# Cosformer attention and SwiGLU: the first batch's denominators computed as one-column products, and the order of the start changed

## The chip, the cores and the metric

The kernel runs on one core of a Trainium2 chip. The core has a matrix engine (TensorE; PE in the profile, with its weight loads on a row of their own, PEld), a vector engine (VectorE, DVE), a scalar engine (ScalarE, ACT), a general engine (GpSimd, POOL) and a queue engine that only issues transfers (SyncE, SP). Each engine works through its own instructions in the order in which the program issues them; engines wait for one another through semaphores. TensorE writes to PSUM, which has eight banks of 512 fp32 columns. The metric is the device time of one execution in microseconds.

## The reference

Attention without softmax for 8 batches, 8 heads, 576 positions and a head size of 64, and behind it a gated feed-forward layer on 4608 rows of 512:

```python
q_p = phi(q, cos_w, sin_w)          # [relu(x)*cos, relu(x)*sin], 128 features
k_p = phi(k, cos_w, sin_w)
kv = np.einsum('bhsf,bhsd->bhfd', k_p, v)
z = np.sum(k_p, axis=2)
num = np.einsum('bhsf,bhfd->bhsd', q_p, kv)
den = np.einsum('bhsf,bhf->bhs', q_p, z)[..., None] + 1e-06
x = num / den                       # heads side by side: rows of 512
xn = x / sqrt(mean(x * x) + 1e-6) * rms_g
out = (silu(xn @ w_gate) * (xn @ w_val)) @ w_out
```

The inner width of the feed-forward layer is 1536. Inputs and output are fp32.

## The kernel before

The feed-forward layer is most of the work: for each block of 512 rows, 12 steps of four gate and four value matmuls (`gval_mm`, L556), SiLU on ScalarE, the product of gate and value on VectorE (L576), and then 48 output matmuls (`out_mm`, L579). Attention of the batches that follow is slipped into these steps. For the first batch there is no block to hide behind, and its order is written out by hand, line by line (L608 to L760); the schedule is manual, so that the order of the calls is the order on each engine. The change lies in that stretch.

In it, batch 0 is handled in these pieces:

- `k_phi` makes the features of k in nine chunks of 64 positions (two halves of the heads stand in the partitions 0 to 63 and 64 to 127, so that a chunk holds four pairs of heads, `hp`, and two groups `g`). VectorE makes the cosine half, ScalarE the sine half of chunks 0 to 7.
- `z0_pe(c)` (L407) adds up the features of a chunk: two matmuls of 64 rows, a matrix of ones against 512 columns. `z0_copy` and `z0_turn` (L415, L418) bring the sums, which lie in a row, into a column: two copies and eight matmuls of one column.
- `g_spread` (L231) spreads the gain `rms_g` over the partitions, three small matmuls for each of four column groups; `gb` is its copy in SBUF.
- `kv0_pe(hp)` (L426) multiplies features by v: 18 matmuls of 64 rows and 64 columns for a pair of heads, the two groups by turns. They fill 64 of 65 columns of each head; the 65th holds the denominator's sum. All four pairs of a group share one bank (`heads0`, in psG). `kvz0_evac` copies a bank to SBUF.
- `q0_phi(eng, j, part)` (L323) makes the features of q tile j (128 rows; four tiles), in two instructions of 256 columns, `i` = 0 and 1, on one engine. `q_tr_pe` transposes a tile on TensorE (eight transposes), and `q0_tr_evac` copies it from PSUM.
- `nd0_pe(j)` (L455) multiplies tile j by the k-v matrices, eight matmuls of 65 columns into both banks of psA, and adds epsilon to the denominators with two matmuls more (L464). `nd_post` divides on VectorE: a reciprocal (L487) and a product (L499).
- `x_sq` sums the squares on ScalarE (L515) and raises them to -1/2 on GpSimd (L520); `x_norm` scales on VectorE (L527), `x_tr_pe` transposes (L546) and `x_tr_evac` copies to `xnT`.
- `unit_mm` (L648) is the first feed-forward work, on one or two tiles at a time.
- `filler(n, bank)` (L601) issues n matmuls of 512 columns on a tile of zeros; nobody reads their result.

Weights, q, k and v of the first batches are loaded by GpSimd's queue, in the order of their calls; the first k by SP's queue.

Of the kernel before, what the change touches and what calls it, by code (L numbers as in the profile page):

```python
# [9 lines left out]
FP32 = mybir.dt.float32  # L10
BF16 = mybir.dt.bfloat16
AF = mybir.ActivationFunctionType
ALU = mybir.AluOpType
# [4 lines left out]
def kernel(  # L18
# [11 lines left out]
    nc = tc.nc  # L30
    B, H, S, D = q.shape
    DM = H * D
    DFF = moe_w_gate.shape[1]
    P = 128
    TB = 512
    HP = H // 2
# [92 lines left out]
    def raw_q0(i):  # L129
        part = raw_tile("q", 0)[:, i * HP * 4 * D : (i + 1) * HP * 4 * D]  # L130
        return part.rearrange("p (hp e) -> p hp e", hp=HP)
# [99 lines left out]
    def g_spread(bank, t):  # L231
        for i in range(3):
            nc.tensor.matmul(  # L233
                bank[:, t * P : (t + 1) * P], lhsT=sel[:, t, :], rhs=g3[:, i, :],
                start=(i == 0), stop=(i == 2),
            )
# [47 lines left out]
    def copy(eng, o, i):  # L284
        if eng is A:
            A.copy(out=o, in_=i)  # L286
        else:
            eng.tensor_copy(out=o, in_=i)  # L288

    def phi(eng, out_ap, in_ap, scale):  # L290
        if eng is A:
            A.activation(out=out_ap, in_=in_ap, func=AF.Relu, scale=scale)  # L292
        else:
            eng.tensor_scalar(  # L294
                out=out_ap, in0=in_ap, scalar1=scale, scalar2=0.0, op0=ALU.mult, op1=ALU.max
            )
# [15 lines left out]
    def qp_of(key):  # L312
        if key not in qp_tiles:
            qp_tiles[key] = four.tile([P, H, F], BF16, name="qp", tag="qp")
        return qp_tiles[key]
# [4 lines left out]
        phi(eng, qp_of((b, j))[:, :, o], raw_q(b)[:, :, j * D : (j + 1) * D], f(9 + j))  # L320


    def q0_phi(eng, j, part):  # L323
        o = slice(0, D) if part == 0 else slice(D, F)
        f = cos_of if part == 0 else sin_of
        for i in range(2):
            c = (2 * j + i) % 4
            phi(
                eng, qp_of((0, j))[:, HP * i : HP * i + HP, o],
                raw_q0(j // 2)[:, :, c * D : (c + 1) * D], f(2 * j + i),  # L330
            )

    def q0_tr_evac(eng, j, bank):
        src = bank.bitcast(BF16).rearrange("p (i h s) -> p i h s", i=2, h=H)
# [24 lines left out]
    def q_tr_pe(b, j, bank):  # L359
        t = qp_of((b, j))  # L360
        dst = bank.bitcast(BF16).rearrange("p (h s) -> p h s", h=H)
        for h in range(H):
            nc.tensor.transpose(dst[:, h, :], t[:, h, :], ident[:, :])  # L363
# [36 lines left out]

    zbank = [psC[1], psV[1]]
    zrow = one.tile([1, 2, HP * F], BF16, name="zrow")
    heads0 = [b[:, 0 : HP * E].rearrange("p (hp e) -> p hp e", e=E) for b in psG]

    def z0_pe(c):  # L407
        for g in range(2):
            lo, hi = 64 * g, 64 * g + 64
            nc.tensor.matmul(  # L410
                zbank[g][:, :], lhsT=ones[lo:hi, :], rhs=kp[lo:hi, c, :, :],
                start=(c == 0), stop=(c == NC - 1),
            )

    def z0_copy(eng, g):  # L415
        copy(eng, zrow[:, g, :], zbank[g][0:1, :])

    def z0_turn():  # L418
        for hp in range(HP):
            for g in range(2):  # L420
                nc.tensor.matmul(
                    heads0[g][:, hp, D:E], lhsT=zrow[:, g, hp * F : (hp + 1) * F],
                    rhs=ones[0:1, 0:1], start=False, stop=False, skip_group_check=True,
                )

    def kv0_pe(hp):  # L426
        for c in range(NC):
            for g in range(2):
                lo, hi = 64 * g, 64 * g + 64
                nc.tensor.matmul(  # L430
                    heads0[g][:, hp, 0:D], lhsT=kp[lo:hi, c, hp, :],
                    rhs=vv0[lo:hi, hp, c * D : (c + 1) * D],
                    start=(hp == 0 and c == 0), stop=(hp == HP - 1 and c == NC - 1),
                    skip_group_check=True,
                )

    def kvz0_evac(eng, g):
        if 0 not in kvzs:
            kvzs[0] = six.tile([P, 2, HP * E], BF16, name="kvzs", tag="kvzs")
        copy(eng, kvzs[0][:, g, :], psG[g][:, 0 : HP * E])  # L440

    def kvz_evac(eng, b):
        kvzs[b] = six.tile([P, 2, HP * E], BF16, name="kvzs", tag="kvzs")
# [8 lines left out]
            )  # L452


    def nd0_pe(j):  # L455
        for h in range(H):
            g, hp = h % 2, h // 2
            nc.tensor.matmul(
                heads[:, g, hp, :], lhsT=qpT[:, h, j * P : (j + 1) * P],
                rhs=kvzs[0][:, g, hp * E : (hp + 1) * E],  # L460
                start=(hp == 0), stop=False, skip_group_check=True,
            )
        for g in range(2):
            nc.tensor.matmul(  # L464
                heads[:, g, :, D], lhsT=eps_ones[:, :], rhs=eps_rows[:, :],
                start=False, stop=True, skip_group_check=True,
            )

    def nd_tails_pe(pair):
# [25 lines left out]
    def nd_div(b, j):  # L495
        xt = xts[count["x"] % NXT]
        count["x"] += 1
        rec = rec_of[(b, j)]
        V.tensor_tensor(  # L499
            out=xt[:, 0:DM].rearrange("p (hp g d) -> p g hp d", g=2, d=D),  # L500
            in0=heads[:, :, :, 0:D],
            in1=rec[:, :, :].unsqueeze(3).to_broadcast([P, 2, HP, D]),
            op=ALU.mult,
        )
        x_of[(b, j)] = xt

    def nd_post(b, j):
        nd_rec(b, j)
        nd_div(b, j)
# [91 lines left out]
    def filler(n, bank):  # L601
        for _ in range(n):
            nc.tensor.matmul(  # L603
                bank[:, :], lhsT=warm[:, 0:P], rhs=warm[:, :], start=True, stop=True
            )


    qbank = [psV[0], psA[:, 0, :], psV[0], psV[1]]  # L608
    g_parts()
    filler(10, psC[1])  # L610
    for c in range(NC):
        k_phi(V, 0, c, 0)
        k_phi(A if c < 8 else V, 0, c, 1)
        z0_pe(c)
        if c < NDT:
            g_spread(psC[0], c)
    kv0_pe(0)
    kv0_pe(1)
    for j in range(2):
        q0_phi(V, j, 0)  # L620
        q0_phi(A, j, 1)
        q_tr_pe(0, j, qbank[j])
    z0_copy(V, 1)
    z0_copy(A, 0)
    q0_tr_evac(V, 0, qbank[0])
    q0_tr_evac(A, 1, qbank[1])
    V.tensor_copy(out=gb[:, :], in_=psC[0][:, :])
    z0_turn()
    kv0_pe(2)
    kv0_pe(3)  # L630
    kvz0_evac(A, 0)
    kvz0_evac(V, 1)

# [44 lines left out]

    HALF = DM // 2
    lo, hi = (0, NDT // 2), (NDT // 2, NDT)
    filler(2, psC[1])
    nd0_pe(0)
    q0_phi(V, 2, 0)
    q0_phi(G, 3, 0)
    q0_phi(A, 2, 1)
    q0_phi(A, 3, 1)
    filler(2, psC[1])
    nd_post(0, 0)  # L690
    q_tr_pe(0, 2, qbank[2])
    filler(1, psC[1])
    x_sq(0, 0)
    load_w(wv, moe_w_val, 8, NNT)
    nd0_pe(1)
    q0_tr_evac(V, 2, qbank[2])
    filler(2, psC[1])
    q_tr_pe(0, 3, qbank[3])
    nd_post(0, 1)
    filler(1, psC[1])  # L700
    nd0_pe(2)
    x_sq(0, 1)
    load_q(1, eng=G)
    load_kv("v", 1, eng=G)
# [3 lines left out]
    filler(1, psG[1])  # L708
    x_tr_pe(0, 0, psC[1], hi)
    x_tr_evac(A, 0, 0, psC[0], lo)  # L710
    x_tr_evac(V, 0, 0, psC[1], hi)
    q0_tr_evac(A, 3, qbank[3])
    x_norm(0, 1)
# [226 lines left out]
```

## Time and profile before

| | |
|---|---|
| three runs | 323.29, 323.61, 324.15 us; median 323.61 |
| the profiled execution | 323.16 us, its span 321.4 us |
| TensorE | busy 317.2 us, 99% of the span, 2310 matmuls |
| VectorE | 184.5 us, 57% |
| ScalarE | 166.2 us, 52% |
| GpSimd | 40.4 us, 13% |
| transfers | 53.76 MB, mean 167 GB/s |

The profile is of one execution. The span runs from its first to its last instruction; the execution's time has 1.76 us more around it. A matmul's row has the duration of the single instruction, and matmuls overlap: two that start 0.06 us apart each have a duration of 0.22. The busy time of TensorE therefore tells little of how far it is from its peak, and the distance between starts tells more. The chain that ended last is followed back from the last instruction; what stands on it sets the end.

### The profile page before, as it was taken

What the parts mean: (1) busy time and instruction counts of PE and PEld (TensorE: products, weight loads), DVE (VectorE), ACT (ScalarE), POOL (GpSimd) and SP (SyncE); (2) the same over time, 40 slices, a digit from 0 to 9 for tenths busy, and PEclk for the clock granted to TensorE, in tenths of its full rate; (3) what the DMA queues carried; (4) which work ended last, traced back from release to release, by engine and by line L of the source; (5) the groups of instructions that cost most, each with busy time, mean ns of one, the idle gap of its engine ahead of it and who ended that gap; (6) DMA issues with size and microseconds to landing.
All of it is one profiled execution on the core that took longest, in us unless ns stands there. A gap on an engine that the chain in (4) does not pass through costs nothing.

```text
span 321.4 us, 6061 instructions
## 1 busy us (share of the span) xinstructions
PE 317.2 (99%) x2310; PEld 162.5 (51%) x2310; DVE 184.5 (57%) x382; ACT 166.2 (52%) x322; POOL 40.4 (13%) x79
## 2 busy tenths in 40 slices
PE   8999999999999999999999999999999999999996
PEld 2689564554454445444544445544544444444444
DVE  7976858668447773777457645781676034204410
ACT  5766756754584466554744575446543333223321
POOL 9771211002001100011001100100011000000000
PEclk9999999999999999999999999999999999999999
DMA  7999999987999989999799859995522500041002
GB/s 234 238 274 268 279 330 159 262 183 189 227 224 203 194 260 189 234 250 168 159 190 230 195 161 200 198 217 162 99 58 42 116 33 0 0 102 31 1 35 98
DMA packets 80091, 53.76 MB, mean 167 GB/s; under 512 B 52234, under 2 KB 74046, under 8 KB 80062
## 3 DMA queue, kind: packets, MB, share of 16 engines
q1 hardware_dynamic: 73110, 41.25, 62.0%
q0 software_dynamic: 6944, 12.13, 15.5%
q8 instruction: 18, 0.29, 0.4%
q14 instruction: 11, 0.09, 0.1%
q10 hardware_dynamic: 8, 0.00, 0.0%
HBM read 37.83 MB, written 9.44 MB: 147 GB/s over the span
## 4 chain that ended last, share of the span: by engine, by line
PE 97%; DVE 1%; ACT 0%; issue 0%; POOL 0%; ACTq 0%
PE psC L579 27%; PE psG L556 27%; PE psV L556 27%; PE psA L449 2%; PE psV L648 2%; PE psG L579 2%; PE psG L648 2%; PE psA L387 2%; PE psC L603 1%; PE psC L410 1%; PE psA L394 1%; PE psA L474 0%; PE psV L363 0%; PE psG L430 0%; PE psC L546 0%; PE psC L233 0%
## 5 line engine op out<-in xcount | busy, mean ns | idle before, releaser
L576 DVE TENSOR_TENSOR hT<-psV,sg 128x512 bf16<-128x512 f32 x100 | 68.9, 689 | 97.7 <-PE psV L556 65.4
L575 ACT ACTIVATE sg<-psG 128x512 f32<-128x512 f32 x100 | 59.2, 592 | 62.3 <-PE psG L556 61.0
L556 PE MATMUL psV<-xnT,wv 128*128 128x512 bf16 x352 | 90.3, 379 | 0.0
L556 PE MATMUL psG<-xnT,wg 128*128 128x512 bf16 x352 | 90.3, 379 | 0.0
L579 PE MATMUL psC<-wo,hT 128*128 128x512 bf16 (+1 forms) x408 | 88.9, 376 | 0.0
L579 PEld LDWEIGHTS <-hT 128*128 128x128 bf16 x456 | 43.0, 98 | 47.8
L556 PEld LDWEIGHTS <-wv 128*128 128x128 bf16 x400 | 39.1, 98 | 47.2
L556 PEld LDWEIGHTS <-wg 128*128 128x128 bf16 x400 | 36.9, 98 | 39.8 <-DVE xnT L288 0.4
L520 POOL TENSOR_TENSOR rs<-ms,mhalf 128x1 f32<-128x1 f32 x36 | 20.5, 571 | 194.6 <-ACT scr L515 194.4
L286 ACT COPY osb<-psC 128x512 f32<-128x512 f32 x32 | 18.8, 586 | 49.9 <-PE psC L579 49.9
L515 ACT ACTIVATE scr<-xt 128x513 bf16<-128x513 f32 x36 | 22.8, 634 | 25.1 <-DVE xt L499 24.4
L527 DVE SCALAR_TENSOR_TENSOR xn<-xt,rs,gb 128x512 bf16<-128x512 f32 (+1 forms) x37 | 27.0, 731 | 9.9 <-POOL rs L520 9.8
L292 ACT ACTIVATE kp<-raw,tab 128x256 bf16<-128x256 f32 (+2 forms) x51 | 28.8, 607 | 2.2 <-DMA raw<-in_k_dram 2.2
L499 DVE TENSOR_TENSOR xt<-psA,rec 128x512 f32<-128x512 f32 x36 | 24.9, 691 | 1.2
L292 ACT ACTIVATE qp<-raw,tab 128x512 bf16<-128x512 f32 (+1 forms) x36 | 23.4, 666 | 1.0 <-DMA raw<-in_q_dram 0.8
L294 DVE TENSOR_SCALAR kp<-raw,tab 128x256 bf16<-128x256 f32 (+2 forms) x53 | 19.9, 423 | 0.5 <-DMA raw<-in_k_dram 0.5
L294 DVE TENSOR_SCALAR qp<-raw,tab 128x512 bf16<-128x512 f32 (+1 forms) x34 | 15.4, 466 | 4.2 <-DMA raw<-in_q_dram 4.2
L449 PEld LDWEIGHTS <-qpT 128*128 128x128 bf16 x224 | 10.5, 97 | 6.7 <-issue 0.7
L556 PE MATMUL psV<-xnT_tail,wv 128*128 128x512 bf16 x48 | 12.3, 379 | 0.0
L556 PE MATMUL psG<-xnT_tail,wg 128*128 128x512 bf16 x48 | 12.3, 379 | 0.0
L449 PE MATMUL psA<-kvzs,qpT 128*128 128x65 bf16 x224 | 11.4, 193 | 0.0
L288 DVE CAST vv<-raw 116x1280 bf16<-116x1280 f32 (+1 forms) x13 | 10.5, 807 | 1.1 <-DMA raw<-in_v_dram 1.1
(100 smaller groups left out, 178.2 us busy)
## 6 DMA issues: line engine op xcount, KB each, us to landing
out_dram<-osb SPq DMA_DIRECT2D x27, 256.0 KB, 2.3
raw<-in_q_dram SPq DMA_DIRECT2D x6, 1024.0 KB, 9.3
raw<-in_k_dram SPq DMA_DIRECT2D x5, 1120.0 KB, 8.5
raw<-in_v_dram SPq DMA_DIRECT2D x5, 1120.0 KB, 9.5
raw<-in_k_dram POOLq DMA_DIRECT2D x2, 1152.0 KB, 19.4
raw<-in_v_dram POOLq DMA_DIRECT2D x2, 1152.0 KB, 16.0
out_dram<-osb SPq DMA_DIRECT2D x17, 128.0 KB, 2.7
wg<-in_moe_w_gate_dram POOLq DMA_DIRECT2D x3, 512.0 KB, 13.6
```

The source lines that it names most:

```text
L286: A.copy(out=o, in_=i)
L292: A.activation(out=out_ap, in_=in_ap, func=AF.Relu, scale=scale)
L294: eng.tensor_scalar(out=out_ap, in0=in_ap, scalar1=scale, scalar2=0.0, op0=ALU.mult, op1=ALU.max)
L449: nc.tensor.matmul(heads[:, g, hp, :], lhsT=qpT[:, h, j * P : (j + 1) * P], rhs=kvzs[b][:, g, hp * E : (hp + 1) * E], start=True, stop=True,)
L499: V.tensor_tensor(out=xt[:, 0:DM].rearrange("p (hp g d) -> p g hp d", g=2, d=D), in0=heads[:, :, :, 0:D], in1=rec[:, :, :].unsqueeze(3).to ...
L515: A.activation(out=scr[:, :], in_=xt[:, 0 : DM + 1], func=AF.Square, scale=1.0 / math.sqrt(DM), accum_out=ms[:, :],)
L520: G.tensor_tensor(out=rs[:, :], in0=ms[:, :], in1=mhalf[:, :], op=ALU.pow)
L527: V.scalar_tensor_tensor(out=xn_of[(b, j)][:, c], in0=x_of[(b, j)][:, c], scalar=rs_of[(b, j)][:, :], in1=gb[:, c], op0=ALU.mult, op1=ALU. ...
L556: nc.tensor.matmul(bank[:, cols[0] : cols[1]], lhsT=w[:, t, n * P : (n + 1) * P], rhs=x[:, t, cols[0] : cols[1]], start=(t == 0), stop=(t ...
L575: A.activation(out=sg[:, :], in_=g[:, 0:TB], func=AF.Silu)
L576: V.tensor_tensor(out=hT[:, n, :], in0=v[:, 0:TB], in1=sg[:, :], op=ALU.mult)
L579: nc.tensor.matmul(bank[:, 0 : cols[1] - cols[0]], lhsT=hT[:, n, j * P : (j + 1) * P], rhs=wo[:, n, cols[0] : cols[1]], start=(n == 0), st ...
```

## The change

The sums of the features of k are formed in a column from the start: `z0_pe(c)` now takes the features as weights and a single column of ones as the moving operand, eight matmuls for a chunk, each into the 65th column of its head. `z0_copy` and `z0_turn` are gone. The heads of pairs 0 and 1 stay in psG, those of pairs 2 and 3 go to psV[1] and psC[1], so that the k-v matrices are copied in two halves for each group. Tile 0 is multiplied and divided in two halves, the first between the k-v products of pairs 0, 1 and those of pairs 2, 3 (`nd0_half`, new). The spreads of the gain come together ahead of the features of k, five fillers stand between the chunks, and the copy of `gb` moves from VectorE to ScalarE. `q0_phi` takes one half of 256 columns at a time; tile 1 gives VectorE three of four, and tiles 2 and 3 are dealt anew between VectorE, ScalarE and GpSimd, which now has one piece instead of two. VectorE's copy of q tile 2 and the product of tile 2 come after the first transposes of x. The transposes of q tile 1 use psC[0] instead of psA.

```diff
-    def q0_phi(eng, j, part):
+    def q0_phi(eng, j, part, i):
...
-    def z0_copy(eng, g):
-        copy(eng, zrow[:, g, :], zbank[g][0:1, :])
-
-    def z0_turn():
         for hp in range(HP):
             for g in range(2):
+                lo, hi = 64 * g, 64 * g + 64
                 nc.tensor.matmul(
-                    heads0[g][:, hp, D:E], lhsT=zrow[:, g, hp * F : (hp + 1) * F],
-                    rhs=ones[0:1, 0:1], start=False, stop=False, skip_group_check=True,
+                    heads0(hp, g)[:, D:E], lhsT=kp[lo:hi, c, hp, :], rhs=ones[lo:hi, 0:1],
+                    start=(hp % 2 == 0 and c == 0), stop=False, skip_group_check=True,
                 )
...
-    def kvz0_evac(eng, g):
+    def kvz0_evac(eng, g, half):
...
-        copy(eng, kvzs[0][:, g, :], psG[g][:, 0 : HP * E])
+        bank = (psG[g], (psV[1], psC[1])[g])[half]
+        copy(eng, kvzs[0][:, g, 2 * E * half : 2 * E * half + 2 * E], bank[:, 0 : 2 * E])
...
+    def nd0_half(half):
+        hps = slice(2 * half, 2 * half + 2)
...
+        V.reciprocal(out=rec0[:, :, hps], in_=heads[:, :, hps, D])
+        V.tensor_tensor(
+            out=x_of[(0, 0)][:, 0:DM].rearrange("p (hp g d) -> p g hp d", g=2, d=D)[:, :, hps],
+            in0=heads[:, :, hps, 0:D],
+            in1=rec0[:, :, hps].unsqueeze(3).to_broadcast([P, 2, 2, D]), op=ALU.mult,
+        )
...
-    qbank = [psV[0], psA[:, 0, :], psV[0], psV[1]]
+    qbank = [psV[0], psC[0], psV[0], psV[1]]
+    half0, half1 = (0, HP // 2), (HP // 2, HP)
     g_parts()
-    filler(10, psC[1])
+    filler(10, psV[0])
+    for t in range(NDT):
+        g_spread(psC[0], t)
     for c in range(NC):
         k_phi(V, 0, c, 0)
         k_phi(A if c < 8 else V, 0, c, 1)
         z0_pe(c)
-        if c < NDT:
-            g_spread(psC[0], c)
+        if 2 < c < NC - 1:
+            filler(1, psV[0])
+    for part in range(2):
+        q0_phi(V, 0, part, 0)
+        q0_phi(A, 0, part, 1)
+    q_tr_pe(0, 0, qbank[0])
     kv0_pe(0)
     kv0_pe(1)
-    for j in range(2):
-        q0_phi(V, j, 0)
-        q0_phi(A, j, 1)
-        q_tr_pe(0, j, qbank[j])
-    z0_copy(V, 1)
-    z0_copy(A, 0)
+    A.copy(out=gb[:, :], in_=psC[0][:, :])
+    q0_phi(V, 1, 0, 0)
+    q0_phi(V, 1, 1, 0)
+    q0_phi(V, 1, 1, 1)
+    q0_phi(A, 1, 0, 1)
+    q_tr_pe(0, 1, qbank[1])
     q0_tr_evac(V, 0, qbank[0])
-    q0_tr_evac(A, 1, qbank[1])
-    V.tensor_copy(out=gb[:, :], in_=psC[0][:, :])
-    z0_turn()
+    kvz0_evac(A, 0, 0)
+    kvz0_evac(V, 1, 0)
+    nd0_pe(0, half0)
     kv0_pe(2)
     kv0_pe(3)
-    kvz0_evac(A, 0)
-    kvz0_evac(V, 1)
+    q0_tr_evac(A, 1, qbank[1])
+    nd0_half(0)
+    kvz0_evac(A, 0, 1)
+    kvz0_evac(V, 1, 1)
...
-    filler(2, psC[1])
-    nd0_pe(0)
-    q0_phi(V, 2, 0)
-    q0_phi(G, 3, 0)
-    q0_phi(A, 2, 1)
-    q0_phi(A, 3, 1)
-    filler(2, psC[1])
-    nd_post(0, 0)
-    q_tr_pe(0, 2, qbank[2])
-    filler(1, psC[1])
+    filler(2, psG[1])
+    nd0_pe(0, half1)
+    q0_phi(G, 3, 0, 0)
+    q0_phi(A, 2, 0, 0)
+    q0_phi(A, 2, 1, 0)
+    q0_phi(V, 3, 1, 1)
+    nd0_half(1)
+    filler(3, psG[1])
     x_sq(0, 0)
     load_w(wv, moe_w_val, 8, NNT)
+    q0_phi(V, 2, 1, 1)
+    q0_phi(V, 2, 0, 1)
     nd0_pe(1)
-    q0_tr_evac(V, 2, qbank[2])
-    filler(2, psC[1])
+    q0_phi(A, 3, 0, 1)
+    q0_phi(A, 3, 1, 0)
+    nd_post(0, 1)
+    filler(1, psG[1])
+    q_tr_pe(0, 2, qbank[2])
+    filler(2, psG[1])
     q_tr_pe(0, 3, qbank[3])
-    nd_post(0, 1)
-    filler(1, psC[1])
-    nd0_pe(2)
     x_sq(0, 1)
...
     x_tr_evac(A, 0, 0, psC[0], lo)
+    q0_tr_evac(V, 2, qbank[2])
+    nd0_pe(2)
     x_tr_evac(V, 0, 0, psC[1], hi)
```

## The prediction

> **What bounds the kernel now.** I read the page first: the share of each engine, then the chain that ended last.
>
> ```profile
> span 321.4 us, 6061 instructions
> PE 317.2 (99%) x2310; PEld 162.5 (51%) x2310; DVE 184.5 (57%) x382; ACT 166.2 (52%) x322; POOL 40.4 (13%) x79
> ...
> PE 97%; DVE 1%; ACT 0%; issue 0%; POOL 0%; ACTq 0%
> ```
>
> TensorE is 97% of the chain; VectorE's 1% can only lie in a short stretch. The chain in order of time, 13 to 17.3 us, finds it:
>
> ```profile
> 13.61 0.70 DVE xt L499
> ...
> 14.39 0.73 ACT scr L515 x2
> 15.13 0.07 issue
> 15.20 0.58 POOL rs L520
> 15.78 0.02 issue
> 15.80 0.50 DVE xn L527
> 16.30 0.05 issue
> 16.35 0.28 PE psC L546 x2
> ```
>
> Tile 0 goes through division, square, power and norm to the first transposes (L546). Behind the first unit (L648) only TensorE follows. So the question is one number: when does unit 0's first gate matmul issue (17.09 us in the timeline)? Later TensorE work is the same in both kernels, and a shift passes to the end.
>
> Third, the timeline of TensorE at the start, for prices (start, duration, group):
>
> ```profile
> 5.56 0.60 PE L410 MATMUL psV<-kp,ones 64*128 64x512 bf16 x1
> 6.10 0.50 PE L233 MATMUL psC<-g,sel 4*128 4x128 bf16 x3
> 6.53 0.46 PE L410 MATMUL psC<-kp,ones 64*128 64x512 bf16 x1
> ...
> 7.19 0.39 PE L410 MATMUL psV<-kp,ones 64*128 64x512 bf16 x1
> 7.51 0.34 PE L233 MATMUL psC<-g,sel 4*128 4x128 bf16 x3
> 7.78 0.39 PE L410 MATMUL psC<-kp,ones 64*128 64x512 bf16 x1
> ...
> 8.60 0.38 PE L410 MATMUL psV<-kp,ones 64*128 64x512 bf16 x1
> 8.81 0.38 PE L410 MATMUL psC<-kp,ones 64*128 64x512 bf16 x1
> ...
> 9.59 0.71 PE L430 MATMUL psG<-vv,kp 64*128 64x64 bf16 x36
> ```
>
> What to see. The 512-column product falls from 0.60 to 0.38 us: TensorE runs at half rate until about 6.7 us, though the granted clock reads 1.0. Undisturbed, a pair follows a pair after 0.215 us (8.60 to 8.81). A round of a pair and three spreads takes 0.59 (7.19 to 7.78), where 0.215 + 3 x 0.06 = 0.395 would do: each change of row size (64 to 4 and back) costs about 0.1 us. The k-v product (64 rows by turns) goes at (0.71 - 0.19)/35 = 14.9 ns.
>
> **The change, along TensorE's order.** Absolute times of the profiled execution; pitches from the rows named.
>
> Fillers end at 5.46 as before. The 12 gain spreads now run together: switch 0.1, eleven at 107 ns (cold; the 6.10 row, three in 0.50) and one warm: 6.80. Before they lay between pairs.
>
> Denominators: 72 one-column products instead of 18 wide ones, plus 8 turning ones that fall away. No row shows 64 rows with one column. Lower bound 13.5 ns (the turning products, one column, one row group, 27 ns each, by two groups); upper 27 ns, no overlap between groups. I take 14.9, the k-v row: same weights, same alternation. So 0.12 us a chunk. The change puts five fillers between chunks: 0.215 each and two switches of 0.1. Switch 0.1, chunks 0 to 3 in 0.48, five times 0.535: 10.05. ScalarE and VectorE finish phi of k at 8.61, so here TensorE is what is late. Switch, transposes of q tile 0 at 10.15 (before 10.23; but then k-v of pairs 0 and 1, 0.54 of issue, had been done).
>
> TensorE goes on: k-v 0, 1 issue 10.70 to 11.24, end 11.41; transposes of tile 1, 11.34 to 11.79. Both v loads have landed (3.01 + 6.5 = 9.5 and 3.71 + 7.3 = 11.0).
>
> Halved VectorE pieces have no row; from two sizes (692 ns for 512 columns, 429 for 260) 1.04 ns a column: 0.29 us for 130 columns, 0.42 for 256. ScalarE likewise (586, 377): 0.27 for 130.
>
> VectorE's phi of q tiles 0, 1 (now five, 0.32 each from 8.53) is over at 10.2. It copies tile 0 from 10.81 (pitch 0.61), then half of k-v, to 11.75. The wait for that copy now stands in front of TensorE's k-v 2, 3: first half of tile 0 at 11.81, epsilon rows with it, ends 12.16. k-v 2, 3: 12.08 to 12.62, end 12.79. VectorE halves: reciprocal 12.21, product 12.44 to 12.87, second k-v copy 12.85 to 13.14. ScalarE: the gain copy (0.59, in the shadow before 9.8), tile 1's copy 12.0 to 13.02, its k-v half to 13.22. Two fillers cover TensorE to 13.14; second half of tile 0 at 13.25, ends 13.60 (before: 13.17 for the whole). VectorE: reciprocal 13.65, product 13.88 to 14.31. Before: 14.30.
>
> Tiles 2 and 3 wait for the second half of q, issued at 4.42 and landed after 8.1, at 12.5, in both kernels. VectorE's piece of tile 3 fits between 13.14 and 13.65: 0.34 alone, 0.57 as in its row beside POOL's phi, which would cost 0.06. ScalarE's two of tile 2 end at 14.1, before it squares.
>
> So dividing by halves pays (only 256 columns after the last k-v), and VectorE's two phi that held the reciprocal to 13.38 before are out of the way; but k-v starts 1.1 us later. These cancel.
>
> From there square and power are the same length: rs at 15.77, norm at 15.80. VectorE's other way there: two phi for tile 2 (14.24 to 14.85), tile 1's rec and product (0.93 from 14.87): 15.80 as well. POOL does one phi less (1.1 us), cover only: its power starts at 15.20 in both; the DMAs it issues behind it (wv, q, v of batch 1) keep their order and time. SP issues nothing in this stretch.
>
> **The tail is where I see the loss.** Before, VectorE copied q tile 2 at 14.22, and tile 2's product ran at 15.81, in TensorE's spare time. Now the copy stands behind both norm halves (end 16.68): 16.62 to 17.31. Behind that copy on VectorE waits the copy of xnT's second half; behind tile 2's product on TensorE, a filler and unit 0. Product 17.36 + 0.29, filler 0.215: unit 0 at 17.87 against 17.09, +0.78. Later, tile 1's transposes waited 0.1 us for their norm (issue could be 17.99, was 18.09); that wait goes. Sum: +0.7 us. The other reordered copies (tile 3's on ScalarE, xnT low half) end before 17.3.
>
> 323.16 for the profiled execution (span 321.4 and 1.76 around it) becomes 323.86; it stands 0.45 under the median of the three runs, so by the median 323.61 + 0.7 = 324.3.
>
> A gain has a ceiling: the first 512 columns of wv, issued at 5.92, land after 11.9 us, at 17.82, and their unit began at 18.33. Under 0.5 us can be won before weights bind.
>
> The Trainium skill, "TensorE: Matmul & The Clock Gate", section "Wait — 56ns, not 53.3ns?", says that starts never come closer than about 25 ns however small the product. The k-v row says 14.9 on average. By the rule 72 products take 1.8 us instead of 1.07, and the sum would be about +1.4 us, slower. I stay with the row; the rule speaks against this change.
>
> **Rivals.**
> 1. Slower: the one-column products don't overlap between row groups. Place: the loop beside phi. At 27 ns they cost 72 x 12.1 ns = 0.87 us more, nothing covers it: +1.57, 325.2. It decides from 19 ns on (+0.97 in all). For it: 27 ns in the turning products. Against: 14.9 in the k-v row.
> 2. Slower: the clock falls. Between 6.8 and 10.1 us only 5 x 0.215 us of full-row work remain, where nine wide pairs ran. If TensorE falls to half rate from about 10 to 13.5, transposes (+0.4), two k-v blocks (+0.45 each), tile products (+0.15) and fillers (+0.43) stretch: +1.9 on top, 326.2. For it: the cold rows until 6.7. Against: before, from 9.6 to 12.1 no full 512-column product ran, and the two fillers at 12.15 took 0.60 us, the warm duration. The same page, section "What's actually happening", has the clock fall after an idle window of about 3.4 us; no run here shows a fall.
> 3. Faster start: the switch doesn't cost anything around fillers, or the products pass faster. Then phi of q tile 0 (9.2) sets its transposes at 9.25, all 0.9 us earlier: -0.2, 323.4; with the ceiling above at most -0.5, 323.1. For it: nothing but that no row has this pair of forms. Against: every change of row size in the timeline shows about 0.1.
> 4. The tail doesn't bind: if VectorE had tile 2's copy done while waiting, the change would be even. Against: its queue is in order, and the norm halves stand ahead.
>
> **Chances and range.** Forecast 0.45, with its own range 323.8 to 324.9: a tenth of a microsecond in each switch moves it by 0.5. Rival 1 0.2, rival 2 0.1, rivals 3 and 4 together 0.25. What a measurement of this kernel tells is about 0.3%, 0.97 us: slower is over 324.58. Of the forecast 0.13 lies there, of the others 0.2 + 0.1 and a little: 0.44. Faster needs more than the ceiling gives: 0.06, for what I have not seen. Same: 0.50. The range takes in rivals 3 and 1 and reaches into 2, with 0.2 for the spread of runs below: 322.9 to 326.0.
>
> **What would show it.** Right: the 72 products with fillers end at about 10.1 us, and the fillers among them take 0.38 us each; tile 0's second product half ends near 14.3, norm starts near 15.8, VectorE's copy of q tile 2 ends at 17.3, unit 0 issues at 17.9. Wrong: z products 2 us or more in sum (rival 1); fillers at 0.6 us after 10 us (rival 2); the norm before 15.3 (rival 3); unit 0 issuing directly behind xnT's copies with tile 2's copy already done (rival 4). Any difference that arises after unit 0 would show that the later stages are not fixed, and make the whole sum wrong.

## The result, and the profile after

The changed kernel took 325.18 us, the median of 8 executions from 324.18 to 325.93; the kernel before took 323.44 us beside it (8 executions, 323.25 to 324.56). The ratio is 1.0046, with a 95% interval from 1.0025 to 1.0066: slower by 0.46%, or 1.7 us. The forecast was 324.3 us and a range from 322.9 to 326.0. The time lies above the 324.58 us from which the prediction calls the kernel slower; it had given that 0.44 and an even time 0.50. And most of the loss arose where rival 2, at 0.1, had put it, not in the tail.

The profiled execution of the changed kernel took 325.46 us. Its page, first the shares of the engines, then the granted clock by slices, then the chain that ended last:

```profile
span 323.7 us, 6133 instructions
...
PE 316.6 (98%) x2326; PEld 164.3 (51%) x2363; DVE 184.6 (57%) x385; ACT 165.7 (51%) x322; POOL 39.3 (12%) x78
...
PEclk9999999999999999999999999999999999999999
...
PE 95%; DVE 2%; DMA 1%; issue 1%; ACT 0%; POOL 0%; DVEq 0%; ACTq 0%
```

TensorE still makes nearly all of the chain, VectorE's share went from 1% to 2%, and the clock's row shows nothing odd. The chain in order of time, from 16.2 to 20 us (start, duration, what):

```profile
16.23 0.73 ACT scr L520 x2
...
17.64 0.88 DVE xn L532 x2
18.52 0.61 DVE qpT L288
...
19.18 0.42 PE psA L447 x8
...
19.70 0.33 PE psG L662 x3
```

It is the chain of before with one piece more: VectorE's copy of q tile 2 (18.52, 0.61 us) and its product (L447) now stand between the norm and unit 0's first gate matmul (L662). That matmul issues at 19.70 us where it issued at 17.09 before, 2.61 us later. The norm begins at 17.64, not at 15.80: 1.84 of the 2.61 us arise ahead of it, and 0.77 behind it.

The 1.84 us are in the timeline of TensorE at the start (start, duration, group; what it waited for in brackets):

```profile
5.56 1.46 PE L233 MATMUL psC<-g,sel 4*128 4x128 bf16 x12
...
8.20 0.61 PE L608 MATMUL psV<-warm 128*128 128x512 bf16 x1
...
10.42 0.61 PE L608 MATMUL psV<-warm 128*128 128x512 bf16 x1
...
11.16 1.03 PE L362 MATMUL psV<-ident,qp 128*128 128x128 bf16 x8
12.13 1.16 PE L419 MATMUL psG<-vv,kp 64*128 64x64 bf16 x36
13.22 0.65 PE L362 MATMUL psC<-ident,qp 128*128 128x128 bf16 x8
...
14.82 0.38 PE L608 MATMUL psG<-warm 128*128 128x512 bf16 x1 [0.16 <-issue]
```

What to see: the fillers among the chunks take 0.61 us each, eight transposes take 1.03 us and the k-v block 1.16 us. In the kernel before these were 0.38, 0.62 and 0.71 us; beside the rows that the prediction shows, its timeline has

```profile
10.23 0.62 PE L363 MATMUL psV<-ident,qp 128*128 128x128 bf16 x8
...
12.15 0.60 PE L603 MATMUL psC<-warm 128*128 128x512 bf16 x2
...
17.09 1.05 PE L648 MATMUL psG<-xnT,wg 128*128 128x128 bf16 x16
```

The second transposes of the changed kernel (0.65 us from 13.22) and its filler at 14.82 (0.38) are at the old durations. So TensorE runs at half rate from its first matmul until about 13.3 us (an estimate from these rows), where the kernel before, with its wide products, had left the half rate at about 6.7. The clock's row on the page has no sign of this: it reads 1.00 here all the time that TensorE hasn't come up yet. One has to read the durations.

Behind unit 0 the difference stays: the products of a later tile come 2.49 us later (40.66 to 43.15 us in the two chains), those near 226 us 2.40 us later, and the end 2.3 us later.

### The profile page after: what moved, and what is told of

Its sections match the earlier page's. It is cut to its first block, busy times and chain, and to the rows that moved or that the text cites. A ratio compares the mean times of both kernels' runs of the same rounds, so it can differ in the third digit from the quotient of the medians.

```text
span 323.7 us, 6133 instructions
## 1 busy us (share of the span) xinstructions
PE 316.6 (98%) x2326; PEld 164.3 (51%) x2363; DVE 184.6 (57%) x385; ACT 165.7 (51%) x322; POOL 39.3 (12%) x78
## 4 chain that ended last, share of the span: by engine, by line
PE 95%; DVE 2%; DMA 1%; issue 1%; ACT 0%; POOL 0%; DVEq 0%; ACTq 0%
PE psV L561 27%; PE psC L584 27%; PE psG L561 26%; PE psA L438 2%; PE psV L662 2%; PE psG L584 2%; PE psG L662 2%; PE psA L386 2%; DMA raw<-in_k_dram 1%; DVE kp L294 1%; PE psA L393 1%; PE psV L608 1%; PE psV L362 1%; PE psA L464 0%; PE psC L362 0%
## 5 line engine op out<-in xcount | busy, mean ns | idle before, releaser
L561 PE MATMUL psG<-xnT,wg 128*128 128x512 bf16 x337 | 88.6, 379 | 0.7 <-issue 0.2
L489 DVE TENSOR_TENSOR xt<-psA,rec 128x512 f32<-128x512 f32 x35 | 24.2, 691 | 1.2
## 6 DMA issues: line engine op xcount, KB each, us to landing
wg<-in_moe_w_gate_dram POOLq DMA_DIRECT2D x3, 512.0 KB, 14.9
```

What stands on the lines that cost most here:

```text
L489: V.tensor_tensor(out=xt[:, 0:DM].rearrange("p (hp g d) -> p g hp d", g=2, d=D), in0=heads[:, :, :, 0:D], in1=rec[:, :, :].unsqueeze(3).to ...
L561: nc.tensor.matmul(bank[:, cols[0] : cols[1]], lhsT=w[:, t, n * P : (n + 1) * P], rhs=x[:, t, cols[0] : cols[1]], start=(t == 0), stop=(t ...
```

## What the mean clock tells of an execution

Each execution leaves its mean granted clock. The profile of `e4_again` below shows one stretch of 3.40 us at half rate, which takes 0.5 x 3.40 / 322 = 0.005 from it, so 0.995 stands for one lost stretch. `e3_tail`'s profile, at 0.989, has two of them on end: its clock by windows of 2 us reads 0.96, 0.50, 0.50, 0.50 and 0.83 from 6 to 16 us, 6.84 us of half rate. A mean of 1.000 stands for none, or for a TensorE that came up late, since the time before that reads 1.00. The 13 executions of the changed kernel (8 above, 5 of the run `e4_again` below) fall into three groups:

| mean clock | executions | time, us |
|---|---|---|
| 0.994 to 0.995 | 8 | 324.14 to 324.90, median 324.42 |
| 0.989 | 2 | 325.69, 325.88 |
| 1.000 | 3 | 325.46, 325.93, 326.12 |

The profile above is of the third group, with its clock up only at 13.3 us; the other two of that group weren't profiled. The groups aren't sharp: one execution of `e1_front16` at 0.995 took 326.12 us, and one of `p4_front16_nofill` at 1.000 took 324.43, 1.2 us above the next of its group. The kernel before read 0.999 or 1.000 in every one of its executions beside the experiments below, from 322.7 to 324.1 us. So the 1.7 us are no fixed cost: the same program loses about 1 us or about 2.3 us, by what the clock does, and the median of 8 falls between the groups.

## The experiments

Theories. *Clock*: the one-column products and the grouped spreads give TensorE too little work per microsecond, so that it comes up late or falls back to half rate, and that makes most of the loss. *Work*: the forecast's sum, in which the clock stays up and the loss is the copy and product of q tile 2 behind the norm. *Serial products*: rival 1, 27 ns for each column product.

Runs `e1` to `e4` ran beside a kernel before with a median of 323.49 us, `p0`, `p1`, `p3` and `p5` beside 323.41, `p2`, `p4` and `p6` beside 323.35, `p7` beside 323.22.

### More fillers in front: e1_front16

```diff
-    filler(10, psV[0])
+    filler(16, psV[0])
```

> The changed kernel with 16 fillers ahead of the gain spreads instead of 10; all else as changed. Theory clock: in the changed kernel TensorE never leaves half rate before about 13 us, because the spreads (4 rows) and one-column products are too little work; six more fillers keep it dense to about 7.2 to 8.0 us, it is at full rate from 8 us at the latest, the fillers among the chunks take 0.38 us instead of 0.61, q tile 0 is transposed near 10.2, unit 0 issues near 17.9, and the time is 324.3, 0.9 under the changed kernel's median of 325.18, with its runs closer together. Rival work: the products, switches and the tail cost what is lost whatever the clock; then six fillers in front only delay, by 1.3 to 2.6 us of TensorE's time less what phi of k hides: 325.5 to 326.5.

324.52 us (10 executions, 323.71 to 326.12), ratio 1.0035, 1.0021 to 1.0049. The mean clock is 1.000 in 9 of 10, and those have a median of 324.35. The timeline of TensorE in its profile:

```profile
8.19 0.20 PE L410 MATMUL psG<-ones,kp 64*128 64x1 bf16 x4
...
8.30 0.19 PE L410 MATMUL psG<-ones,kp 64*128 64x1 bf16 x4
...
8.67 0.39 PE L608 MATMUL psV<-warm 128*128 128x512 bf16 x1
...
9.18 0.39 PE L608 MATMUL psV<-warm 128*128 128x512 bf16 x1
...
11.21 0.62 PE L362 MATMUL psV<-ident,qp 128*128 128x128 bf16 x8
11.76 0.71 PE L419 MATMUL psG<-vv,kp 64*128 64x64 bf16 x36
...
18.85 1.05 PE L662 MATMUL psG<-xnT,wg 128*128 128x128 bf16 x16
```

This is the changed kernel with its clock up, as the forecast had assumed. A chunk's eight column products follow the last chunk's after 0.105 us (8.19 to 8.30, and the next at 8.40), 13 ns for each: the serial theory (27 ns) falls. A filler and a chunk go by in 0.51 us (8.67 to 9.18; the forecast had 0.535, with two switches of 0.1 us). From the transposes of q tile 0 (11.21) to unit 0 (18.85) it takes 7.64 us, and the forecast had 10.15 to 17.87, 7.72. The part of the expectation on the start was wrong: the six fillers more push the transposes from 10.15 to 11.21 by themselves, and so the version isn't faster.

### No fillers among the chunks: e2_nofill

```diff
         z0_pe(c)
-        if 2 < c < NC - 1:
-            filler(1, psV[0])
```

> The changed kernel without the five fillers among the chunks of k. Theory clock: the start stays at half rate as now (or falls further behind), since even with them it was at half rate; but TensorE is then not late for phi of k: q tile 0 transposed at 9.4 instead of 11.2, gaining at most 1.8 us there and losing part of it where the later pieces run at half rate for longer: 324.0 to 325.5, transposes of eight at 1.0 us. Rival work: the fillers and their ten switches are pure cost, 2.1 us at full rate, of which 0.9 lies on the path: 324.2, and eight transposes take 0.61 us.

324.43 us (10 executions, 323.91 to 325.15), 1.0034, 1.0024 to 1.0045. Five executions had a clock of 0.995 (median 324.12), three 0.988 or 0.989 (median 325.09), two 1.000 (324.37 and 324.49). One of the last two was profiled; its timeline of TensorE:

```profile
9.17 1.04 PE L362 MATMUL psV<-ident,qp 128*128 128x128 bf16 x8 [0.25 <-POOL eps_rows L227]
10.14 1.16 PE L419 MATMUL psG<-vv,kp 64*128 64x64 bf16 x36
```

The transposes take 1.04 us as the clock theory had it, not 0.61. They begin 2 us earlier than in the changed kernel's profile (9.17 for 11.16), and yet the time falls only to 324.4: the half rate stays, in this execution through the transposes and the first k-v block at least, and the fillers' place is partly taken by waits (0.25 us ahead of the transposes).

### The tail in another order: e3_tail

```diff
     x_tr_evac(A, 0, 0, psC[0], lo)
-    q0_tr_evac(V, 2, qbank[2])
-    nd0_pe(2)
     x_tr_evac(V, 0, 0, psC[1], hi)
+    q0_tr_evac(V, 2, qbank[2])
     q0_tr_evac(A, 3, qbank[3])
-    x_norm(0, 1)
-    nd_post(0, 2)
     filler(1, psG[1])
     unit_mm(0, wg, by_rows=True)
+    nd0_pe(2)
+    x_norm(0, 1)
+    nd_post(0, 2)
```

> The changed kernel with VectorE's copy of q tile 2 behind the copy of xnT's upper half, and tile 2's product behind unit 0's gate matmuls instead of ahead of them. Theory of the forecast (the tail binds, 0.78 us): unit 0 issues behind the last transposes of x and one filler, 0.6 to 0.7 us earlier than in the changed kernel in the same state of the clock: 324.5. Rival: the tail doesn't bind and all of the loss lies ahead of the norm: 325.2.

324.72 us (6 executions, 324.13 to 326.05), 1.0045, 1.0028 to 1.0062. Compared within the group of one lost stretch: 324.26 (3) for 324.42 (8), no gain that can be told. The timeline of TensorE shows why the 0.6 us expected didn't come:

```profile
18.85 1.05 PE L662 MATMUL psG<-xnT,wg 128*128 128x128 bf16 x16
...
20.36 0.40 PE L551 MATMUL psC<-ident,xn 128*128 128x128 bf16 x4 [0.18 <-DVE xn L532]
20.59 0.61 PE L662 MATMUL psV<-xnT,wv 128*128 128x128 bf16 x8
```

and that of VectorE:

```profile
18.75 0.29 DVE L288 COPY xnT<-psC 128x256 bf16<-128x256 bf16 x1 [0.46 <-PE psC L551]
18.96 0.68 DVE L288 COPY qpT<-psV 128x1024 bf16<-128x1024 bf16 x1
19.56 0.74 DVE L532 SCALAR_TENSOR_TENSOR xn<-xt,rs,gb 128x512 bf16<-128x512 f32 x1
```

Unit 0 issues 1.44 us behind the norm (17.41), not 2.06: the 0.6 us is won there. But the copy has only moved by one place on VectorE, and tile 1's norm (19.56) waits behind it now. Tile 1's transposes wait for that norm, and unit 0's second half (wv, 20.59) comes 3.18 us behind the first norm, exactly as in the changed kernel (17.64 to 20.82). In both places tried behind the norm the copy costs its 0.6 us.

### The changed kernel once more: e4_again

> The changed kernel once more, for a second profile. Theory clock: its eight runs so far lie in two groups (324.2 to 324.9 and 325.5 to 325.9) because the moment at which TensorE comes to full rate falls differently in each execution; runs again from 324.2 to 325.9, and a profile whose fillers after chunk 3 take either 0.38 us (then unit 0 near 17.9 and the time near 324.4) or 0.61 us (unit 0 near 19.5, near 325.6). Rival: one state only, the profile again at half rate to 13 us while the time is at the low end.

Nothing is edited. 324.43 us (5 executions, 324.14 to 326.12), 1.0043, 1.0024 to 1.0062. Four of five have a clock of 0.995. The profiled one took 324.21 us; its timeline of TensorE:

```profile
8.40 0.39 PE L608 MATMUL psV<-warm 128*128 128x512 bf16 x1
...
8.91 0.61 PE L608 MATMUL psV<-warm 128*128 128x512 bf16 x1
...
9.65 1.03 PE L362 MATMUL psV<-ident,qp 128*128 128x128 bf16 x8
10.62 1.16 PE L419 MATMUL psG<-vv,kp 64*128 64x64 bf16 x36
```

and its busy time by windows (us; busy of PE, PEld, DVE, ACT, POOL with counts; then PEclk, the share of the transfers, GB/s):

```profile
6.00:8.00 2.00, 2.00 (x59) 1.36 (x55) 1.72 (x6) 1.99 (x6) 2.00 (x3) 1.00 1.07 273
8.00:10.00 2.00, 2.00 (x31) 1.07 (x31) 2.00 (x8) 1.62 (x5) 1.66 (x6) 0.73 1.21 220
10.00:12.00 2.00, 2.00 (x46) 1.71 (x44) 1.19 (x4) 0.69 (x3) 1.19 (x3) 0.50 1.11 323
12.00:14.00 2.00, 2.00 (x56) 1.59 (x55) 1.28 (x5) 1.44 (x4) 0.94 (x1) 0.92 1.24 209
```

Here the fall is in the record. A clock of 0.73 from 8 to 10 us is 0.92 us at full and the rest at half rate, so it falls at 8.92; 0.92 from 12 to 14 us puts the rise at 12.32. That is 3.40 us of half rate. This execution had come up early (its twelve spreads took 0.84 us for 1.46, its fillers 0.39), so q tile 0's transposes began at 9.65, ahead of the 10.15 forecast; then they, the first k-v block and part of the second transposes were slow, and the norm began at 16.37, 0.57 later than before. With 0.77 in the tail, unit 0 is 1.34 late (18.43). So 324.2 to 324.4 us is the forecast's number, by another sum: an earlier start, and a stretch of half rate in its place.

### Without the transposing transfers: p0_before and p1_after

From here on, in every run, plain copies of the same tiles take the place of the DMA transposes of the later batches, so the values of those batches aren't the reference's.

```diff
-        nc.sync.dma_start_transpose(
-            out=qpT[:, :, j * P : (j + 1) * P], in_=t[:, :, :].rearrange("p h f -> p (h f)")
-        )
+        nc.sync.dma_start(out=qpT[:, :, j * P : (j + 1) * P], in_=t[:, :, :])
...
-        nc.sync.dma_start_transpose(out=x_dst(b, j), in_=xn_of[(b, j)][:, :])
+        nc.sync.dma_start(
+            out=x_dst(b, j), in_=xn_of[(b, j)][:, :].rearrange("p (t s) -> p t s", s=P)
+        )
```

> The kernel before with the 59 DMA transposes of the later batches (q tiles from batch 2 on, normed tiles from batch 1 on, tails) replaced by plain DMA copies of the same size, so that the later batches' values are wrong; the first 40 us are untouched. A reference for the parts that follow. All theories: the chain behind unit 0 is TensorE's, so the time stays within 0.5 of 323.5 and unit 0 issues near 17.1 us, with a mean clock of 1.0.

323.39 us (11 executions, 322.93 to 324.05) for 323.41, ratio 1.0003, 0.9994 to 1.0012: the base of the parts below. In its profile the first k-v block waits 0.56 us for its load of v, and the norm (16.20) and unit 0 (17.49) come 0.40 us later than in the profile of the kernel before. So landmarks of single profiles can differ by that much where the median times agree.

> The changed kernel with the same plain copies in place of the DMA transposes (later batches' values wrong). Theory clock: slower than its reference by 0.9 where the mean clock is 0.995 and by 2.2 where it is 0.989 or where TensorE never left half rate in the start; by 1.0 to 2.0 in the median. Rival: a loss that comes from the later stages (the transposes' transfers, say) would be gone or of another size here.

325.3 us (6 executions, 324.12 to 326.29), 1.0056, 1.0035 to 1.0078. The groups are those of the changed kernel: 324.12 and 324.14 at 0.995, 325.17 and 325.43 at 0.989, 326.01 and 326.29 at 1.000. So the loss doesn't come from the DMA transposes of the later batches.

### The column products alone: p3_cols

The kernel before with the sums formed in columns and the row copies and turning products gone; the banks, the order and the tail stay as they were.

```diff
     def z0_pe(c):
-        for g in range(2):
-            lo, hi = 64 * g, 64 * g + 64
-            nc.tensor.matmul(
-                zbank[g][:, :], lhsT=ones[lo:hi, :], rhs=kp[lo:hi, c, :, :],
...
+                lo, hi = 64 * g, 64 * g + 64
                 nc.tensor.matmul(
+                    heads0[g][:, hp, D:E], lhsT=kp[lo:hi, c, hp, :], rhs=ones[lo:hi, 0:1],
...
-    z0_copy(V, 1)
-    z0_copy(A, 0)
...
-    z0_turn()
```

> The kernel before with one part of the change alone, the one-column products (into the single bank of each group), without row copies and turning products; gain spreads, fillers, phi and tail as before; plain copies in place of the DMA transposes. Theory clock: between 5.5 and 9 us only spreads and one-column products run, so TensorE falls back to half rate (or never leaves it) and the transposes and k-v products of 9 to 13 us take up to twice as long, 1.0 and 1.16 us instead of 0.61 and 0.71: 0.4 to 1.5 slower than its reference, mean clock 0.995 or less in most runs. Rival work: the products are cheaper than the wide ones and two copies fall away: 0.3 to 0.5 faster.

324.55 us (7 executions, 323.86 to 325.56), 1.0040, 1.0025 to 1.0055, with clocks of 1.000 (3), 0.995 (1) and 0.988 or 0.989 (3). The timeline of TensorE in its profile (324.55 us):

```profile
5.76 0.49 PE L233 MATMUL psC<-g,sel 4*128 4x128 bf16 x3
...
9.74 1.16 PE L414 MATMUL psG<-vv,kp 64*128 64x64 bf16 x36 [0.83 <-DMA vv<-in_v_dram]
...
11.66 1.06 PE L359 MATMUL psA<-ident,qp 128*128 128x128 bf16 x8
12.66 1.10 PE L414 MATMUL psG<-vv,kp 64*128 64x64 bf16 x36
13.91 0.38 PE L589 MATMUL psC<-warm 128*128 128x512 bf16 x1 [0.16 <-issue]
```

The half rate lasts until about 13.6 us, with the order, the tail and the banks of before. TensorE has less to do (the first k-v block waits 0.83 us for its load), and the kernel is 1.1 us slower. This one part gives 1.1 of the 1.9 us that `p1_after` loses.

### The tail alone: p5_before_tail

```diff
     nd0_pe(1)
-    q0_tr_evac(V, 2, qbank[2])
...
-    nd0_pe(2)
     x_sq(0, 1)
...
     x_tr_evac(A, 0, 0, psC[0], lo)
+    q0_tr_evac(V, 2, qbank[2])
+    nd0_pe(2)
```

> The kernel before with one part of the change alone: VectorE's copy of q tile 2 and tile 2's product moved behind the first transposes of x; plain copies in place of the DMA transposes. Theory of the forecast: VectorE's copy stands behind the norm's halves, unit 0 issues 0.78 us later, 0.1 comes back at tile 1's transposes: 0.7 slower than its reference. Rival: the tail doesn't bind, the idle time of VectorE there takes the copy: no difference.

323.71 us (11 executions, 323.28 to 324.55), 1.0014, 1.0004 to 1.0023; that is +0.32 us over `p0_before`, and +0.45 by the ratio (0.13 to 0.74). The clock is 0.999 or 1.000. The chain in order of time:

```profile
15.88 0.88 DVE xn L523 x2
16.77 0.61 DVE qpT L288
...
17.42 0.42 PE psA L454 x8
...
17.95 1.05 PE psG L646 x16
```

The pieces are those that the forecast listed, and unit 0 comes 2.07 us behind the norm; in `p0_before` it is 1.29 (16.20 to 17.49), as in the kernel before (15.80 to 17.09). The price of 0.78 us at unit 0 is exact. At the second half of unit 0 it is down to 0.65 us (3.18 us behind the norm for 2.53), where the forecast, after the 0.1 us that it gave back, had 0.7. In the time about 0.3 to 0.45 us are left, though the interval doesn't exclude 0.7. Where the rest is won back I didn't find.

### Wide sums in the new order: p2_wide

The changed kernel with the wide sums of before in psA, their two row copies and the turning products in two parts, and no fillers among the chunks.

```diff
     def z0_pe(c):
-        for hp in range(HP):
+        for g in range(2):
+            lo, hi = 64 * g, 64 * g + 64
+            nc.tensor.matmul(
+                psA[:, g, :], lhsT=ones[lo:hi, :], rhs=kp[lo:hi, c, :, :],
...
+    z0_copy(V, 1)
+    z0_copy(A, 0)
...
     q_tr_pe(0, 1, qbank[1])
+    z0_turn((0, 1))
```

> The changed kernel with the denominators formed as before (wide products of ones against 512 columns, into psA, two row copies, eight turning products in two parts) and no fillers among the chunks; banks, halves, order of phi and the tail as changed; plain copies in place of the DMA transposes. Theory clock: the wide products keep TensorE dense, it comes to full rate by 8 us in every execution and never falls, the mean granted clock is 1.0 in all runs and eight transposes take 0.61 us; the tail's loss remains (0.3 to 0.7), the extra row copies cost VectorE perhaps 0.2 more: 323.7 to 324.3, with runs closer together than the changed kernel's. Rival: the loss beyond the tail comes from the halves, the banks and the waits between TensorE and VectorE, whatever form the denominators have: 324.4 to 326, as the changed kernel, and in groups.

324.79 us (5 executions, 324.05 to 324.93), 1.0036, 1.0023 to 1.0050; the clock is 1.000 in all five. I had expected 323.7 to 324.3; the median lies in the range of the rival, 324.4 to 326, which put the loss down to the halves, the banks and the waits of the new order. In the profiled execution, the shortest (324.05 us), q tile 0's transposes begin at 9.43 at full rate, and the timeline of VectorE has the row copy in the way:

```profile
10.29 0.67 DVE L288 CAST zrow<-psA 1x512 bf16<-1x512 f32 x1
10.89 0.67 DVE L288 COPY qpT<-psV 128x1024 bf16<-128x1024 bf16 x1
```

The 0.6 us of copy of one row holds tile 0's copy, and the chain of this execution runs through ScalarE's row copy (10.04, 0.47 us) and the copy of `gb` behind it; the norm begins at 16.19 and unit 0 at 18.26. So no fall shows with wide sums, but in the new order their row copies are on the path. The three executions near 324.8 have no profile, and a late rise there can't be told from no loss; that stays open. Whether the new order costs anything without the row copies is for the next run to tell.

### Dense work in front, nothing among the chunks: p4_front16_nofill, p6_cols_front16, p7_spread_mid

`p4` is the changed kernel with 16 fillers in front and none among the chunks; `p6` is `p3` with 16 fillers in front; `p7` is `p4` with the spreads ahead of the last six of the 16.

```diff
-    filler(10, psV[0])
+    filler(16, psV[0])
...
-        if 2 < c < NC - 1:
-            filler(1, psV[0])
```

> The changed kernel with 16 fillers in front and none among the chunks, plain copies in place of the DMA transposes. Theory clock: full rate by 8 us; if the sparse 2 us of spreads and column products don't bring it down, q tile 0 is transposed near 9.4 to 9.9 and unit 0 follows 7.66 later (the sum of the forecast from there), near 17.1 to 17.6: 323.5 to 324.0, better than with 16 fillers and five more (324.5) and than without either (324.4); if they bring it down, near 324.4 with a clock of 0.995. Rival work: no difference to the run without fillers, or slower by the time of the six, 324.4 to 325.5.

323.89 us (12 executions, 322.78 to 324.48), 1.0005, 0.9993 to 1.0018. Six have a clock of 1.000, with a median of 322.99 (five from 322.78 to 323.20, one at 324.43); six 0.995, with a median of 323.93. One lost stretch thus costs 0.94 us, by these medians. The profile is of the first group (322.91 us); its timeline of TensorE:

```profile
9.17 0.62 PE L358 MATMUL psV<-ident,qp 128*128 128x128 bf16 x8 [0.27 <-POOL eps_rows L227]
9.76 0.71 PE L415 MATMUL psG<-vv,kp 64*128 64x64 bf16 x36
...
17.16 1.05 PE L658 MATMUL psG<-xnT,wg 128*128 128x128 bf16 x16
```

With the clock up, the transposes begin a microsecond earlier than before, the norm at 15.09 (before 15.80), and unit 0 at 17.16 (before 17.09): what the new order wins ahead of the norm, 0.71 us, the tail takes. Beside `p0_before` (16.20 and 17.49) the norm is 1.11 us earlier and unit 0 0.33. So the halves, the banks and the new order cost nothing in sum while the clock is up (322.99 for 323.35), which speaks against the rival of `p2_wide`. The norm doesn't come earlier still because its chain is VectorE's now: the second half of q lands at 12.66 us, and phi, the second half of tile 0's division, two phi more and tile 1's division follow one another up to 15.09.

> The kernel before with the one-column products alone, and 16 fillers in front instead of 10; plain copies in place of the DMA transposes. Theory clock: the six fillers make the start dense to 7.0 to 8.0 us, TensorE is at full rate from then on and stays there; the loss of the run with ten fillers (324.55, 1.1 over its reference) is gone for the most part: 323.2 to 323.8, mean clock 1.0, k-v products of 36 in 0.71 us. Rival work: six more fillers only push TensorE back by 1.3 us or more: 324.6 to 325.8.

323.95 us (12 executions, 322.80 to 326.27), 1.0020, 1.0003 to 1.0037. Five at 1.000 have a median of 323.20, six at 0.994 or 0.995 one of 324.29 (1.09 us more), one at 0.989 took 326.27. The profile is of the second group; its busy time by windows (columns as above):

```profile
8.00:10.00 2.00, 1.31 (x75) 1.13 (x75) 1.80 (x6) 1.90 (x5) 1.87 (x7) 1.00 1.21 210
10.00:12.00 2.00, 2.00 (x61) 1.78 (x55) 1.18 (x2) 0.67 (x1) 0.95 (x3) 0.76 1.11 331
```

TensorE has work for 1.31 of 2 us from 8 to 10, and the clock falls at 11.0. It is back at 14.4 (0.89 from 14 to 16 us), after 3.40 us again. So more fillers in front don't keep the clock up here: seven of twelve executions lost a stretch, and the median misses the 323.2 to 323.8 expected.

> The run with 16 fillers in front and none among the chunks, with the gain spreads between the tenth filler and the eleventh instead of behind the sixteenth; plain copies in place of the DMA transposes. Theory clock: the sparse stretch behind the last filler is shorter by the 0.8 us of the spreads, so fewer executions fall back to half rate: most runs at a clock of 1.0 and 322.8 to 323.2, median 323.0, 0.1% faster than before. Rival: the spreads in the middle spoil the stretch that brings TensorE up, so that some executions reach full rate only 3.4 us later and wait for six cold fillers: a second group at 324.5 to 325.5.

323.38 us (12 executions, 322.60 to 324.34), 1.0004, 0.9992 to 1.0017. Eleven have a clock of 1.000 (median 323.33), one 0.995 (324.34). The same fillers, dealt differently, lose a stretch in 1 of 12 executions where `p4` did in 6 of 12; twelve executions each suggest a difference and don't settle it. I had expected a median of 323.0. But the undisturbed time is 0.3 us above that of `p4`, and the kernel is level with before. No version beat the kernel before by more than its measurement tells.

## Why the prediction was right and wrong

Landmarks, in us from the start of the span, from the timelines and chains of one profiled execution each (for the forecast, its own numbers):

| | before | forecast | after | e4_again | e1_front16 | p4_front16_nofill |
|---|---|---|---|---|---|---|
| transposes of q tile 0 | 10.23 | 10.15 | 11.16 | 9.65 | 11.21 | 9.17 |
| first norm | 15.80 | 15.80 | 17.64 | 16.37 | 16.79 | 15.09 |
| unit 0's first gate matmul | 17.09 | 17.87 | 19.70 | 18.43 | 18.85 | 17.16 |
| end of the span | 321.4 | | 323.7 | 322.4 | 323.2 | 321.1 |

`p0_before`, the base of `p4` with its plain copies, has 10.70, 16.20, 17.49 and 321.9 in these rows.

- **The step that failed** is the silent one: that TensorE would be at full rate from 6.8 us on, as before. The forecast took the time at which the half rate ended over from a kernel whose wide products (nine pairs of 512 columns) kept TensorE dense, and the change removes just these. In the changed kernel's profile the rise came at about 13.3 us, in `e4_again` it came early and was lost again from 8.92 to 12.32. `p3_cols` shows that the column products do it alone. `e1` shows that work in front of them changes how often it happens: 1 of 10 executions shows a lost stretch, where all 13 of the changed kernel were disturbed if those at 1.000 came up late. `p7` beside `p4` points the same way, and `p6` still loses a stretch in 7 of 12.
- **Rival 2** named the place and the mechanism, at a chance of 0.1, and its time of 326.2 is near that of the group at 1.000 (325.46 to 326.12), whose one profile is a late rise. Its form was one of several: a single fall costs 0.94 (`p4`) or 1.09 us (`p6`), not 1.9, and the rise that doesn't come wasn't thought of. The row held against it, the fillers at 12.15 at full rate behind 2.5 us without a 512-column product, said less than it was taken for. That time was full of back-to-back k-v products and transposes, and shorter than the 3.40 us of a stretch, so it says nothing of a start with one-column products.
- **Rival 1** falls: 13 ns for each product, by `e1`; 14.9 was taken, 13.5 was the lower bound. Its price of 325.2 us is the measured median, by chance. The Trainium skill's floor of about 25 ns between starts ("TensorE: Matmul & The Clock Gate", section "Wait — 56ns, not 53.3ns?") isn't seen where two row groups take turns.
- **The switches** of 0.1 us and the round of 0.535 hold (0.51 in `e1`).
- **The sum from the transposes to unit 0** holds where the clock is up: 7.64 in `e1` for 7.72. So the halves of tile 0, ScalarE's copies and the phi dealt anew are right in sum; the single terms weren't compared.
- **The tail** holds at unit 0 to 0.01 us (2.06 in the changed kernel, 2.07 forecast and in `p5`), but of the 0.7 us of time that the forecast gave the move 0.3 to 0.45 were measured (interval by the ratio 0.13 to 0.74). That the shift at unit 0 passes whole to the end was too strong by about 0.3 us: in the changed kernel it is 2.61 at unit 0 and 2.3 at the end.
- **Rival 3** had its condition wrong, since the switches do cost 0.1 us each. A faster start does come, by other ways: in `e4_again` because the clock was up some 1.2 us sooner than forecast (transposes at 9.65), in `p4` because no fillers stand among the chunks (9.17). `p4` with the clock up takes 322.99 against 323.35; most of its start is taken by the tail.
- **The time**: the 324.3 forecast is what the changed kernel takes in its commonest group (324.42), but by errors of opposite sign: a start that is 0.5 us earlier than forecast, a tail worth less, and a lost stretch of nearly 1 us. Of the eight executions of the result four are in this group and four at 325.46 to 325.93, so that the median, 325.18, falls between. That the forecast's number was met by one group is luck.

What stays open: what exactly the clock goes by; whether all executions of the changed kernel at a clock of 1.000 came up late (one of the three was profiled); what the three slower executions of `p2_wide` lost; and the 0.3 us or so that come back behind unit 0.

## What to carry to other kernels

When a change takes dense TensorE work out of the start and puts small products in its place, count the full-row work that is left in each few microseconds before taking over any duration from the old profile: a microsecond of TensorE saved can cost a clock that comes up 6 us later (about 13.3 us for 6.7). Read the rate from the duration of a known matmul (0.38 or 0.61 us for 512 columns), since the page's clock row shows full clock for a TensorE that hasn't come up. And group executions by their mean clock before comparing medians; a median over two groups is a number that no execution need have.

## What the runs showed of the hardware

- The clock falls though TensorE is never idle for long. In `e4_again` it was busy in all of 6 to 8 us (2.00 of 2.00), and from the rise on (5.5 us, by its spreads) to the fall at 8.92 only five fillers started, at most 5 x 0.215 = 1.1 us of full-row work in 3.4 us. The Trainium skill, "TensorE: Matmul & The Clock Gate", section "What's actually happening", has the clock fall after an idle window of about 3.4 us. A length of 3.40 us is found here too, as that of the half rate from the fall to the rise; idleness isn't, in the sense of the profile's busy time.
- Fillers in 72% of a stretch may not be enough for the rise; this is an estimate, not a record. In the changed kernel's profile the fillers end at 5.56 and spreads with four rows follow until 7.0. If stretches of 3.40 us follow one another without a gap, as the two in `e3_tail` do, one ended at 6.5, two stretches ahead of the rise at 13.3, with fillers in 2.46 of its 3.40 us, and the clock did not come up.
- The same program falls into different groups by execution: the rise came at about 13.3 us in one profile of the changed kernel and by 5.5 us in another. The same section says that the window runs freely and doesn't start with the kernel, which would give this; no run here steers the window, so that the phase is the cause isn't shown.
- Two row groups by turns pass one-column products at 13 ns each, half of the 27 ns of one group in the turning products of before. At half rate a chunk's eight take the same 0.105 us (7.08 to 7.18 in the changed kernel's timeline), so the rate can't be read from them.
